# Linear attention, second pass: softmax work of a tile moved into the output products of the tile in front, and loads and sums at the pass boundary spread

## The chip, the cores and the metric

The kernel runs on one core of a Trainium2 chip. The metric is the device time of one execution in microseconds (us), the median of several runs. The core has a matrix engine (TensorE, PE in the profile; PEld is its weight loading), a vector engine (VectorE, DVE), a scalar engine (ScalarE, ACT), a general engine (GpSimd, POOL), and SyncE (SP), which here issues DMA transfers. Each engine works through its own queue in order and waits at an instruction until what it needs has been signalled.

## The reference

Four layers are applied to x (2048 rows of 512), each as a residual: A, B, A, B. Both layers A use one set of weights, both layers B another. The change lies in layer A:

```python
qkv = (x @ wqkv) ...                       # 32 heads of 16
pq = einsum(q, w_phi); pk = einsum(k, w_phi)
phi_q = concat([softmax(pq), softmax(-pq)])  # over the 16 features of a head
phi_k = concat([softmax(pk), softmax(-pk)])
kv = einsum(phi_k, v); z = sum(phi_k)        # over all 2048 rows
o = (phi_q @ kv) / (phi_q @ z + 1e-6)
x = x + o @ wo                               # x normalized (layernorm) before qkv
```

Layer B is a causal attention in four segments of 512 rows with a running memory; it follows each layer A.

## The kernel before, in words

Rows are worked in 16 tiles of 128. Products with full precision are made of three products of split operands (a high part and a low part), so a 128x512 projection is twelve matmuls over four blocks of the inner dimension.

Layer A has two passes. `pass1` (L746) goes through four segments of four tiles. It makes keys, values and query projections, the features of the keys, and adds up the key-value sums `kva` (`kv`, L825: 64 small matmuls for two tiles, then one addition on DVE). For most tiles the query projection is written to DRAM and comes back in the second pass (`load_q`, L956); for the last segment the queries stay on chip. The end of pass 1 is written out by hand (L893 to L954): two query and four key projections, two value tiles (the generator `rest`, steps 6 and 7), query projections of tiles 2 and 3, the two halves of the sums `kv(0)` and `kv(1)`, and the load of the output weights `awo` (eight DMAs of 256 KB; `pace()` at L458 makes SyncE wait for the last matmul issued so far). The output weights go into two of the four buffers `w8`, which also hold value weights and, for some segments, normalized rows.

The features of a tile are made in steps, each with a function of its own. `differences` (L638) subtracts the extremes of every head, two operations on POOL, into a tile of tag `P4`. `exp` (L648) is one operation on ACT. `scale_q` (L661) sums on DVE (`es`), makes a factor on DVE (`rr`) and multiplies half of the tile by it on POOL. After that PE can transpose the tile (`transposed`, L962, into `lg`, copied by ACT), and `products` (L976) multiplies it with the key-value sums and divides by the denominators on DVE (`r`, then `U`).

`pass2` (L992) goes through the 16 tiles. In step i of the loop, for a tile in the middle, the order of issue is: turn the output of tile i-1 (transposes on PE, casts on ACT, low parts on DVE), the exponential of tile i+2, the transposes of tile i+1, the products of tile i, the differences of tile i+3, sums and factor of tile i+2, the load of tile i+4, the load of the residual rows, and the twelve output products of tile i-1 with their addition on DVE and the store. Towards the end some steps handle two tiles at once (`NT - 5` and the like: step 10 makes the differences of tiles 13 and 14, step 11 those of tile 15).

Order is kept by hand: wrappers named `Ordered` chain all operations of DVE, ACT, POOL and SyncE in the order in which the program issues them, and `held` does so for PE. Generators yield between pieces, and the first 104 pieces of pass 2 are interleaved with the opening of the following layer B (`STEPS`, L47): its weight loads, the normalization of its first segment, in which POOL refines the root (`refine`, L380) and PE transposes the rows (`columns`, L393). The rest of pass 2 runs in early slots of layer B.

All operations on DVE, ACT, POOL and SyncE pass through one helper, so that the profile puts them at L155; matmuls stand at L177, transposes at L181 and L187.

Of the kernel before, what the change touches and what calls it, by code (L numbers as in the profile page):

```python
# [101 lines left out]
def interleave_kernel(ctx, tc, x_in, a_wqkv, a_wphi, a_wo, b_wq, b_wk, b_wv, b_wo, b_beta,  # L102
# [572 lines left out]
    class LayerA:  # L675
# [70 lines left out]
        def pass1(self, first):  # L746
# [44 lines left out]
            for n, s in enumerate(SEGS):  # L791
# [30 lines left out]
                    self.pqs[i] = dtile((P, D), nm("pq"))  # L822
                    sync.dma_start(out=self.pqs[i], in_=pq)

                def kv(t2, n=n, v=v, es=es):  # L825


                    pk = PS(("mx", "my")[t2], 1)[:, 0 : 8 * VW].rearrange("p (g e) -> p g e", e=VW)
                    for g in range(8):
                        for t in range(2 * t2, 2 * t2 + 2):  # L830
                            for j in range(4):
                                h = 4 * g + j
                                mm(pk[32 * j : 32 * j + 32, g, :], lhsT=es[t][:, 32 * h : 32 * h + 32],
                                   rhs=v[:, t, VW * h : VW * h + VW], start=(t == 2 * t2), stop=(t == 2 * t2 + 1),
                                   tile_position=(0, 32 * j))
                    yield
                    if n == 0 and t2 == 0:
                        dve.tensor_copy(kva, pk)
                    else:
                        dve.tensor_tensor(out=kva, in0=pk, in1=kva, op=ADD)  # L840
                    yield
# [65 lines left out]
                for i, (at, t) in enumerate(tiles):  # L907
                    for j, _ in enumerate(qproj(t, e, later) if at else kproj(t, e)):
                        if j == 2 and i > 1:
                            scaled(i - 2)  # L910
                        yield
                    if at:
                        begun(t)
                    if i > 0:
                        exp(e[sum(tiles[i - 1])])
                    if i == 2:
                        yield from late
                for i in (6, 7):
                    for j in range(4):
                        next(rest)  # L920
                        if j == 2:
                            scaled(i - 2)
                        yield
                    if i == 6:
                        exp(e[sum(tiles[i - 1])])
                        yield from kv(0)
                for _ in qproj(2, e, later):
                    yield
                begun(2)
                add = kv(1)  # L930
                next(add)
                pace()
                self.wo = load_w("awo")
                yield from add
                KN = self.KN = sp.tile([P, 8, 4, VW], F32, tag="KN", bufs=1, name=nm("KN"))
                den = kva[:, :, DH]
                dve.tensor_scalar(den, den, 0.5e-6, None, op0=ADD)
# [54 lines left out]
        def pass2(self):  # L992
# [2 lines left out]

            transposed = self.transposed
            self.rest = []
            for i in range(NT):
                soon = [i + 2] if i < NT - 5 else [i + 2, i + 3] if i == NT - 5 else [i + 3]
                soon = [n for n in soon if 2 < n < NT]  # L1000
                if i > 0:
                    if i <= NT - 4:
                        if i < NT - 4:
                            oT = turn_halves(self.o)
                        else:
                            oT = turn([self.o[:, c * P : (c + 1) * P] for c in range(NC)])
                        yield
                    for n in soon if i != 1 else ():
                        exp(self.e[n])
                    self.o = T2("ot", OT) if NT - 4 <= i else T2("U", UU)  # L1010
                    if i > 2:
                        yield from transposed(i + 1)
                    yield from self.products(i)
                for n in [i + 3] if i < NT - 6 else [i + 3, i + 4] if i == NT - 6 else [i + 4]:
                    if 3 < n < NT:
                        self.e[n] = differences(*self.raw.pop(n))
                for n in soon if i != 1 else ():
                    scale_q(self.e[n])
                for n in [i + 4] if i < NT - 7 else [i + 4, i + 5] if i == NT - 7 else [i + 5]:
                    self.load_q(n)  # L1020
                if i < NT - 4:
                    ahead = residual(self.xsrc, i, ("ot", OT))
                else:
                    self.rest.append(self.o)
                if 0 < i <= NT - 4:
                    steps = out_proj(x, self.xdst, i - 1, oT, self.wo, i < 3)
                    if i < 3:
                        for _ in range(2):
                            next(steps)
                            yield  # L1030
                        yield from transposed(i + 1)
                    if i == 1:
                        for n in soon:
                            exp(self.e[n])
                    yield from steps
                if i == 1:
                    scale_q(self.e[i + 2])
                x = ahead
# [622 lines left out]
```

## Time and profile before

| | us |
|---|---|
| median of three runs | 1315.0 (1313.81 to 1315.15) |
| the profiled execution: its own time | 1319.74 |
| its span | 1318.0 |
| PE busy | 1265.2 (96%) |
| PE weight load busy | 978.4 (74%) |
| DVE busy | 1078.5 (82%) |
| ACT busy | 836.6 (63%) |
| POOL busy | 753.7 (57%) |
| mean granted clock of PE | 0.995 |

The page of the profile counts busy time by engine and follows back the chain of work that ended last. In rows of the timeline, the columns are start, duration, engine, line, operation, output and inputs with their sizes, and a count where rows are merged; in brackets stands how long the engine was idle before it and what ended that. Rows of the chain have start, duration and what ran. In rows of the view by windows, each engine's busy time has its instruction count in brackets, and granted PE clock, share of the DMA engines and GB/s follow. Matmuls overlap, and their ends are modelled, so that a busy PE is not PE at its peak.

Names: `es` and `rr` are the sums and the factor of a query tile, `P` its features, `tb` and `mmq` a loaded query tile and its extremes, `lg` the transposed tile in PSUM, `KN` the key-value sums, `U` and `ot` the output of a tile, `oh` and `ol` its turned halves, `w` and `oh` in `g<-w,oh` the output products.

### The profile page before, as it was taken

The numbers are of one execution on the slowest core, as the hardware profiler recorded it, in microseconds if no ns is written. First come the engines' busy times: TensorE is split into PE (matmuls) and PEld (weight loads), VectorE is DVE, ScalarE is ACT, GpSimd is POOL, SyncE is SP. The second block draws the span as 40 slices with busy tenths as digits, with TensorE's granted clock in tenths as the row PEclk, the third lists the DMA queues.
The fourth block names the chain that finished last, engine by engine and source line by source line (L and its number), as shares of the span: only waits on it lengthen the run. The fifth ranks groups of instructions, "written<-read, shape, count | busy, mean of one in ns | idle before, by whom it ended". The sixth has DMA issues, their size and how long they took to land.

```text
span 1318.0 us, 42698 instructions
## 1 busy us (share of the span) xinstructions
PE 1265.2 (96%) x16832; PEld 978.4 (74%) x16832; DVE 1078.5 (82%) x3523; ACT 836.6 (63%) x1232; POOL 753.7 (57%) x1122
## 2 busy tenths in 40 slices
PE   8999989999999999999999999899999999999987
PEld 7887767777777777777668887677777777777765
DVE  5766858788998998998857768687899899898995
ACT  6546434547778788776644434464678868877754
POOL 0668845425657667666324447562356766766653
PEclk9999989999999999999999999899999999999999
DMA  6398167545555545545451101855546545544432
GB/s 211 110 354 268 62 203 232 169 120 145 182 172 140 160 120 145 159 134 156 130 168 57 65 34 53 266 181 158 143 129 209 174 127 152 144 131 119 122 83 81
DMA packets 134423, 196.64 MB, mean 149 GB/s; under 512 B 15440, under 2 KB 61648, under 8 KB 133456
## 3 DMA queue, kind: packets, MB, share of 16 engines
q1 hardware_dynamic: 133408, 193.80, 48.7%
q8 instruction: 134, 2.20, 0.7%
q14 instruction: 65, 0.53, 0.1%
q10 hardware_dynamic: 816, 0.11, 0.1%
HBM read 101.05 MB, written 39.85 MB: 107 GB/s over the span
## 4 chain that ended last, share of the span: by engine, by line
PE 69%; DVE 17%; DMA 4%; POOL 3%; SPq 2%; issue 2%; ACT 2%; DVEq 0%; POOLq 0%; ACTq 0%
PE g L177 54%; PE lg L177 6%; PE g L181 3%; PE mx L177 3%; DVE es L155 3%; DVE U L155 2%; POOL P L155 2%; SPq L155 2%; DVE g L155 2%; DVE mx L155 2%; PE my L177 1%; DVE my L155 1%; DMA w<-awo 1%; DMA wqk<-wqk 1%; DMA e<-ta 1%
## 5 line engine op out<-in xcount | busy, mean ns | idle before, releaser
L155 ACT ACTIVATE P<-lg 128x1024 f32<-128x1024 f32 x316 | 324.3, 1026 | 98.0 <-PE lg L177 77.1
L155 POOL TENSOR_SCALAR_AFFINE_SELECT P<-P 128x256 f32<-128x256 f32 (+1 forms) x448 | 189.9, 442 | 234.7 <-ACT P L155 207.8
L155 DVE CUSTOM_DVE_ANT_0 g<-g,mask 128x128 f32<-128x128 f32 (+3 forms) x392 | 189.5, 539 | 10.1 <-PE g L177 9.7
L155 DVE CUSTOM_DVE_ANT_0 mx<-mx,mask 128x512 f32<-128x512 f32 (+2 forms) x316 | 159.2, 504 | 42.1 <-PE my L177 33.8
L177 PE MATMUL g<-hh,wqk 64*128 64x512 f32 (+1 forms) x960 | 183.9, 393 | 4.2 <-SPq L155 2.5
L177 PE MATMUL g<-w,oh 64*128 64x512 f32 (+2 forms) x848 | 164.8, 384 | 8.2 <-DMA w<-awo 5.1
L155 DVE CUSTOM_DVE_ANT_0 my<-my,mask 128x512 f32<-128x512 f32 (+2 forms) x316 | 164.2, 520 | 0.0
L177 PE MATMUL lg<-e,e 64*128 64x512 f32 (+1 forms) x1010 | 146.2, 343 | 7.8 <-ACT P L155 7.8
L177 PE MATMUL g<-P,v 128*32 128x128 f32 (+3 forms) x2064 | 151.6, 433 | 0.1
L155 DVE DVE_READ_ACCUMULATOR2_ANT mxs<- 128x1 f32 x1024 | 145.1, 142 | 0.0
L177 PE MATMUL g<-w,hh 64*128 64x512 f32 (+1 forms) x672 | 142.1, 394 | 2.8 <-SPq L155 1.3
L177 PEld LDWEIGHTS lg<-e,e 64*128 64x128 f32 x1010 | 92.8, 184 | 52.6 <-ACT P L155 20.2
L177 PEld LDWEIGHTS g<-hh,wqk 64*128 64x128 f32 (+1 forms) x960 | 100.6, 185 | 23.6 <-SPq L155 4.8
L177 PEld LDWEIGHTS g<-w,oh 64*128 64x128 f32 (+1 forms) x848 | 95.3, 188 | 27.7 <-DMA w<-awo 6.6
L177 PEld LDWEIGHTS g<-P,v 128*32 128x32 f32 x2064 | 64.8, 109 | 61.3 <-issue 53.8
L155 ACT COPY tb<-g 128x512 f32<-128x512 f32 (+1 forms) x132 | 71.2, 576 | 53.9 <-PE g L177 53.6
L177 PE MATMUL g<-hl,wqk 64*128 64x512 f32 (+1 forms) x480 | 102.7, 390 | 0.0
L177 PE MATMUL g<-w,ol 64*128 64x512 f32 (+2 forms) x424 | 101.2, 381 | 0.0
L177 PEld LDWEIGHTS g<-w,hh 64*128 64x128 f32 (+1 forms) x672 | 83.5, 186 | 18.0 <-SPq L155 2.2
L177 PE MATMUL g<-w,hl 64*128 64x512 f32 (+1 forms) x336 | 88.8, 391 | 0.0
L155 POOL TENSOR_TENSOR ta<-tb,ta 128x512 fp32r<-128x512 f32 x60 | 76.2, 1290 | 16.3 <-ACT ta L155 13.3
L177 PE MATMUL mx<-e,e 63*128 63x256 f32 (+3 forms) x323 | 82.2, 318 | 2.4 <-DVE r L155 1.5
(170 smaller groups left out, 2937.7 us busy)
## 6 DMA issues: line engine op xcount, KB each, us to landing
e<-ta SPq DMA_DIRECT2D x384, 128.0 KB
wqk<-wqk SPq DMA_DIRECT2D x128, 256.0 KB
x<-x SPq DMA_DIRECT2D x48, 256.0 KB
pq<-tb SPq DMA_DIRECT2D x24, 256.0 KB
tb<-pq SPq DMA_DIRECT2D x24, 256.0 KB
x<-xr SPq DMA_DIRECT2D x22, 256.0 KB
xr<-x SPq DMA_DIRECT2D x20, 256.0 KB
x<-in SPq DMA_DIRECT2D x16, 256.0 KB
```

What stands on the lines that cost most here:

```text
L155: i = f(*a, **k)
L177: return held(nc.tensor.matmul(*a, **k))
L181: return held(nc.tensor.transpose(*a))
```

## The change

Three edits in layer A. Both layers A run them.

In `kv`, a new argument lets the sums of two tiles be made in two halves.

At the end of pass 1, each of the two value tiles starts with a `pace()` and the issue of half of the loads of the output weights. The sums of tiles 0 and 1 are made in two halves inside the second value tile, after its first and its third block; those of tiles 2 and 3 in two halves, one inside the query projection of tile 2 and one after it. Before, all sums of a pair were made in one piece, and all loads were issued behind the second pair.

In pass 2, from step 2 on, the exponential, the sums and the factor that step i+1 would have issued are issued in step i, ahead of the last block of its output products: in a step in the middle those of tile i+3 behind the differences of tile i+3 in that step. Step 2 still issues those of tile 4 at the old places as well. The differences, the transposes, the products and the loads of query tiles stay where they were.

```diff
-                def kv(t2, n=n, v=v, es=es):
+                def kv(t2, n=n, v=v, es=es, split=False):
...
+                        if split and g == 3:
+                            yield
...
+                self.wo = []
+                wsteps = bring(self.wo, "awo")
+                sums = [kv(t2, split=True) for t2 in range(2)]
                 for i in (6, 7):
+                    pace()
+                    for _ in range(2):
+                        next(wsteps)
                     for j in range(4):
                         next(rest)
                         if j == 2:
                             scaled(i - 2)
                         yield
+                        if i == 7 and j in (0, 2):
+                            next(sums[0])
+                            yield
                     if i == 6:
                         exp(e[sum(tiles[i - 1])])
-                        yield from kv(0)
-                for _ in qproj(2, e, later):
+                    else:
+                        yield from sums[0]
+                for j, _ in enumerate(qproj(2, e, later)):
+                    if j == 1:
+                        next(sums[1])
                     yield
                 begun(2)
-                add = kv(1)
-                next(add)
-                pace()
-                self.wo = load_w("awo")
-                yield from add
+                yield from sums[1]
+                for _ in wsteps:
+                    pass
...
+            def due(i):
+                soon = [i + 2] if i < NT - 5 else [i + 2, i + 3] if i == NT - 5 else [i + 3]
+                return [n for n in soon if 2 < n < NT]
+
             for i in range(NT):
-                soon = [i + 2] if i < NT - 5 else [i + 2, i + 3] if i == NT - 5 else [i + 3]
-                soon = [n for n in soon if 2 < n < NT]
+                soon = due(i) if i < 3 else ()
...
                     if i == 1:
                         for n in soon:
                             exp(self.e[n])
-                    yield from steps
+                        yield from steps
+                    else:
+                        for _ in range(1 if i == 2 else 3):
+                            next(steps)
+                            yield
+                        for n in due(i + 1):
+                            exp(self.e[n])
+                        for n in due(i + 1):
+                            scale_q(self.e[n])
+                        yield from steps
```

## The prediction

> **What bounds the kernel now.** I read the page first, then the chain of waits around the two places that the change touches, then the timelines of single engines there.
>
> ```profile
> span 1318.0 us, 42698 instructions
> PE 69%; DVE 17%; DMA 4%; POOL 3%; SPq 2%; issue 2%; ACT 2%; DVEq 0%; POOLq 0%; ACTq 0%
> ```
>
> Most of the chain is TensorE (PE), so an edit off PE counts only where PE waits. In the second pass it does. One tile there, in the chain of waits of the first layer A:
>
> ```profile
> 197.32 1.14 DVE es L155
> ...
> 199.21 1.07 POOL P L155
> 200.32 0.71 PE lg L187 x16
> ...
> 203.04 1.14 DVE es L155
> ```
>
> From `es` to the next `es` is 5.72 us, a closed loop: sums of tile i+2 (DVE), factor (POOL), transposes of that tile (PE), products of the tile before it behind them in PE's queue, division by the denominators (DVE), next sums. PE's own work in that tile is shorter:
>
> ```profile
> 200.32 0.71 PE L187 MATMUL lg<-ident,P 64*128 64x64 f32 x16 [0.53 <-POOL P L155]
> 202.05 0.73 PE L177 MATMUL g<-w,oh 128*128 128x512 f32 x2
> 205.06 0.27 PE L187 MATMUL mx<-ident,U 64*128 64x64 f32 x1
> 206.03 0.71 PE L187 MATMUL lg<-ident,P 64*128 64x64 f32 x16 [0.51 <-POOL P L155]
> ```
>
> The twelve output products take 202.05 to 205.06, 3.0 us. The wait ahead of the transposes is 0.51, so PE is busy 5.2 of 5.72 us. No way of moving the sums can win more than 0.5 us a tile.
>
> The other place is the start of the second pass, where PE waits for the output weights:
>
> ```profile
> 170.74 4.51 SPq L155 DMA_DIRECT2D w<-awo  x8
> 177.57 1.38 PE L177 MATMUL g<-w,oh 128*128 128x512 f32 x3
> 181.66 1.65 PE L177 MATMUL g<-w,oh 128*128 128x512 f32 x3 [2.71 <-DMA w<-awo]
> 187.14 0.36 PE L187 MATMUL mx<-ident,U 64*128 64x64 f32 x1
> 815.46 4.41 SPq L155 DMA_DIRECT2D w<-awo  x8
> 822.29 0.74 PE L177 MATMUL g<-w,oh 128*128 128x512 f32 x2
> 825.92 1.65 PE L177 MATMUL g<-w,oh 128*128 128x512 f32 x3 [1.62 <-DMA w<-awo]
> 831.40 0.36 PE L187 MATMUL mx<-ident,U 64*128 64x64 f32 x1
> ```
>
> The first four rows are the first layer A, the others the second. The clock fell with the wait; in the view by windows the third number from the end is the granted PE clock, 0.66:
>
> ```profile
> 180.00:190.00 10.00, 8.34 (x70) 6.09 (x71) 2.99 (x7) 3.58 (x5) 2.70 (x4) 0.66 0.68 242
> ```
>
> **Part 1: output weights earlier.** Between the first output product of tile 0 and the next tile's turn (177.57 to 187.14) stand twelve products and one tile's transposes: 3.0 + 0.65 = 3.65 us of work took 9.57. The excess is 5.9 us, 2.7 of it waiting and 3.2 mostly the low clock. In the second layer A: 831.40 - 822.29 - 3.65 = 5.5 us.
>
> In the first layer the eight loads now go out in two lots from the last key projection on, two value tiles and a query projection (twelve products, 3.0 us each) ahead of the old place: 9 us earlier, longer than PE waits, so all 5.9 us come back. In the second, the four `w8` buffers hold the value weights and the normalized rows until the last value product (both operands are `w` in the row below), so SyncE's loads stand waiting for it, and so would anything behind them on that queue; nothing is, until pass 2's first load of query rows.
>
> ```profile
> 808.27 3.04 PE L177 MATMUL g<-w,w 128*128 128x512 f32 x12
> 812.20 1.52 POOL L155 TENSOR_TENSOR P<-P,es 128x512 f32<-128x512 f32 x1 [1.48 <-DVE es L155]
> 814.03 1.27 PE L177 MATMUL my<-v,P 128*32 128x17 f32 x128
> ```
>
> The last value product ends near 811.3 in either order, 4 us ahead of the old first issue. Old, the last weight landed 10.5 us after the first issue (815.46 to 825.92); new, that gives 821.8, ahead of PE's need at 822.3 (823.5 with part 2). So that wait goes too; if the loads took 2 us longer, half of it would stay.
>
> **Part 2: key-value sums spread.** They are the same products. The first half of tiles 2 and 3's sums now stands after six of the twelve products of the next query projection and needs the scaled tile that POOL finishes at 812.20 + 1.52 = 813.72. PE gets there near 812.6, waits 1.1, and still has both halves of the sums (0.6 each) and six products (1.5) to do: it ends near 816.4 where the old sums ended at 815.3. So +1.2 in the second layer (0 if POOL is earlier, +2 if the query projection's later steps slip as well); in the first PE is idle around these sums already, and I take nothing. Part 1 and 2 together: -5.9 - 5.5 + 1.2 = -10.2 us.
>
> **Part 3: exponential, sums and factor one tile ahead.** The old loop is cut: the factor is ready a tile before the transposes ask. But look at POOL's queue. It runs in order. In tile i it subtracts the extremes of tile i+3 (two operations), and, old, then multiplied by the factor of tile i+2. Now the exponential of tile i+3 (ScalarE), its sums (DVE) and its factor (POOL) all follow the subtraction of the same tile in the same step, and the subtraction of tile i+4 is queued behind that factor. That is a new closed loop. The trace has all its links in one run, in the first pass:
>
> ```profile
> 144.18 2.09 POOL P L155 x2
> 146.30 1.07 ACT P L155
> 147.39 1.23 DVE es L155
> ```
> ```profile
> 149.37 1.06 POOL L155 TENSOR_TENSOR P<-P,rr 128x512 f32<-128x512 f32 x1 [0.95 <-DVE rr L155]
> 150.40 1.06 POOL L155 TENSOR_TENSOR P<-U,mm 128x512 f32<-128x512 f32 x1
> ```
>
> Subtraction to next subtraction: 150.40 - 144.18 = 6.22 us, against 5.72 old. DVE passes the delay on: the addition that ends each tile's output rows, and the low halves of the next, are queued behind the sums that wait for the exponential; PE then waits before the output products, about 1 us a tile (6.22 less its 5.2). On ScalarE the exponential now stands ahead of the next turn's two casts, which need PE's turn behind the output products and so come no earlier; that adds nothing.
>
> Length of the stage, from the turn of tile 1 to the transposes of tile 13. Old:
>
> ```profile
> 191.74 1.02 ACT L155 COPY P<-lg 128x1024 f32<-128x1024 f32 x1 [2.39 <-PE lg L187]
> 223.86 0.49 POOL L155 TENSOR_TENSOR st<-st 128x4 f32<-128x4 f32 x2 [0.59 <-ACT st L155]
> 225.49 1.06 POOL L155 TENSOR_TENSOR P<-tb,mmq 128x512 f32<-128x512 f32 x1
> 246.73 0.71 PE L187 MATMUL lg<-ident,P 64*128 64x64 f32 x16 [0.41 <-POOL P L155]
> 891.26 0.71 PE L187 MATMUL lg<-ident,P 64*128 64x64 f32 x16 [0.40 <-POOL P L155]
> ```
>
> 246.73 - 187.14 = 59.6 us, and 891.26 - 831.40 = 59.9 in the second layer. New: tile 5's exponential follows the copy at 191.74, so 1.02 + 1.09 (146.30 to 147.39) + 1.98 (147.39 to 149.37) + 1.03 later POOL starts the subtraction of tile 6 at 196.86, 9.7 after the turn. From there seven rounds of 6.22 bring it to tile 13: 43.5. The refinement of layer B's norm, six small operations, stands once in POOL's queue: 225.49 - 223.86 = 1.6. After that comes the double step of tiles 13 and 14, where the chain runs on through DVE and PE:
>
> ```profile
> 247.21 0.69 DVE L155 TENSOR_TENSOR hl<-g,hh 128x512 fp32r<-128x512 f32 x1
> 247.81 0.68 DVE L155 TENSOR_TENSOR ot<-g,ot 128x512 f32<-128x512 f32 x1
> 270.54 1.22 DVE L155 TENSOR_REDUCE es<-P 128x64 f32<-128x1024 f32 x1
> 272.35 0.69 DVE L155 CUSTOM_DVE_ANT_0 g<-g,mask 128x512 f32<-128x512 f32 x1
> ```
>
> Both subtractions take 4.2 (twice 2.09), the second exponential 1.1, the sums of tile 14 1.8 (270.54 to 272.35, sums and factor), three more 128x512 operations on DVE at 0.6 from start to start 1.8, then on PE twelve products 3.0 and the turn 0.5 (5.2 less 3.0 less the 1.7 from 200.32 to 202.05): 12.4. New stage 9.7 + 43.5 + 1.6 + 12.4 = 67.2: +7.6 and +7.3, +15 in both layers. In return the sums of tile 15, the row at 270.54, leave the opening of layer B, where DVE has no pause:
>
> ```profile
> 270.00:280.00 10.00, 9.95 (x88) 7.01 (x90) 9.72 (x38) 3.26 (x5) 3.52 (x3) 1.00 0.21 65
> ```
>
> At most 1.8 us a layer (DVE is busy 9.72 of 10), nothing if PE (9.95) is the limit; I take -1, -2 in both.
>
> **The clock.** The low clock of the 0.66 row came with a wait of 2.7 us and cost up to 3.2 beyond it. The new stage makes two such holes a layer: behind the refinement, 1.0 + 1.6 = 2.6 us, and behind the double step, about 3. Part of PE's slowness there goes into its 1 us of slack. I take one fall a layer at 1.5: +3 (ends 0 and +12.8, four falls at full price). [...]
>
> **Sum.** -10.2 + 15 - 2 + 3 = +5.8 us. Against the profiled execution's own 1319.74 (span 1318.0) that is 1325.5; the median of the three runs, 1315.0, lies 4.7 lower, and I carry the difference over: 1320.8, or 1321.
>
> **Rivals.** *A, POOL does not hold the loop* (the subtraction runs ahead of the factor, or the exponential is issued late enough that neither loop closes). Then PE's 5.2 us decide: nine tiles at -0.5 in two layers, -9, with -10.2 and -2: 1294, about 1296 with some loss at the close. For it: the edit does cut the old loop. Against: all POOL operations are chained in the order of the program. It decides from a POOL round under 5.7 us. This is the case on the other side, faster. 0.17.
> *B, the loop binds but the close is cheap*: if tiles 10 to 12 hide the double step, a layer loses seven times 0.5 and little more, 4 us: -10.2 + 8 - 2 = -4, 1311. 0.13.
> *C, the clock falls twice a layer* at nearly full price: +10 in place of +3, about 1328. For it: the one wait of this size that is quoted brought a fall. 0.20.
> *E, the clock stays whole*: PE's holes are cut short by the work that fills them (transposes, turn), and the term of 3 is nothing: -10.2 + 15 - 2 = +2.8, 1318. For it: the holes are an estimate from sums of links, each of which may overlap a little more. 0.15. [...]
> *D, the change does not do what it says* in the second layer, the loads finding no buffer before the sums: then its 5.5 stay lost, 1326.5; I put it inside C's range. Late loads of the query rows, which POOL already waits for in places, would lengthen some rounds by up to a microsecond; also inside.
> Forecast itself (the loop binds, one fall a layer): 0.35, with its own range of 1314 to 1326.
>
> **Numbers.** Range 1309 to 1331: it takes in B, E, the forecast and C, and leaves out A and little else. A measurement of this kernel can tell about 0.2%, 2.6 us, from no change. Faster by more (under 1312.4): A and part of B, 0.22. Within it: part of E, the lower end of the forecast and the rest of B, 0.14. Slower: 0.64.
>
> **What would show it.** The waits for `w<-awo` gone at both places and the clock whole there. In the second pass, POOL's subtractions 6.2 us apart, with an idle stretch ahead of each factor, and PE's wait moved from the transposes (for POOL) to the output products (for DVE). The stage from turn 1 to transposes 13 near 67 us; sums of tile 15 before layer B opens; a clock under 1 in the last tiles. I am wrong if tiles are 5.2 to 5.7 us apart, or if PE's waits are not on that path.

## The result and the profile after

| | before | after |
|---|---|---|
| median, us | 1315.1 (1313.81 to 1316.16, 4 runs) | 1325.5 (1322.36 to 1327.33, 4 runs) |
| ratio, 95% interval | | 1.0077 [1.0055, 1.0099] |
| profiled execution, own time | 1319.74 | 1325.99 |
| span | 1318.0 | 1324.1 |
| mean granted clock of PE | 0.995 | 0.995 |

The change makes the kernel 10.4 us slower. Its page gives the span and the shares of the chain:

```profile
span 1324.1 us, 42698 instructions
PE 73%; DVE 13%; POOL 5%; ACT 3%; DMA 2%; issue 2%; SPq 1%; DVEq 0%; POOLq 0%; ACTq 0%
```

DMA fell from 4% to 2% of the chain, and about half of that is the row of the output weights (`w<-awo`), which had 1.1% of the span before and is gone. POOL rose from 3% to 5%.

**The pass boundary.** From the timelines of SyncE and PE, first layer A, then the second:

```profile
157.50 4.66 SPq L155 DMA_DIRECT2D w<-awo  x8
167.43 0.67 PE L177 MATMUL my<-v,P 128*32 128x17 f32 x56 [1.07 <-POOL P L155]
177.72 1.67 PE L177 MATMUL g<-w,oh 128*128 128x512 f32 x6
181.54 0.27 PE L187 MATMUL mx<-ident,U 64*128 64x64 f32 x1
812.42 4.39 SPq L155 DMA_DIRECT2D w<-awo  x8
815.44 0.67 PE L177 MATMUL my<-v,P 128*32 128x17 f32 x56 [1.23 <-POOL P L155]
825.72 1.67 PE L177 MATMUL g<-w,oh 128*128 128x512 f32 x6
829.56 0.27 PE L187 MATMUL mx<-ident,U 64*128 64x64 f32 x1
```

The six first output products now run in one piece. The turn of tile 1 starts at 181.54, where it started at 187.14: 5.6 us won. In the second layer it is 829.56 against 831.40; this layer's start came 1.7 us late, so 3.5 are won there. PE's new wait of about a microsecond for the scaled key tile stands in both layers.

**The second pass.** POOL's timeline in the first layer A (`P<-P,rr` is the factor, `P<-tb,mmq` the first subtraction of the next tile):

```profile
190.43 1.06 POOL L155 TENSOR_TENSOR P<-P,rr 128x512 f32<-128x512 f32 x1 [1.48 <-DVE rr L155]
191.44 1.06 POOL L155 TENSOR_TENSOR P<-tb,mmq 128x512 f32<-128x512 f32 x1
...
196.62 1.06 POOL L155 TENSOR_TENSOR P<-P,rr 128x512 f32<-128x512 f32 x1 [3.10 <-DVE rr L155]
...
211.32 1.06 POOL L155 TENSOR_TENSOR P<-tb,mmq 128x512 f32<-128x512 f32 x1 [1.25 <-DMA tb<-pq]
```

In a plain round the factors follow each other at 6.19 us, with POOL idle about 3 us (2.99 to 3.10) ahead of each: it has subtracted tile i+3, and waits for ScalarE and DVE to bring the same tile's factor, while the next subtraction is queued behind that. Once in the first layer and twice in the second (0.41 and 1.17 us) the subtraction also waits for its query tile. The chain shows why that one is late:

```profile
202.58 0.69 DVE xr L155
...
203.29 2.39 DMA x<-xr
...
206.12 5.06 DMA tb<-pq
...
211.32 1.06 POOL P L155
```

The load of the next query tile stands on SyncE's queue behind the store of a finished row tile, and that store waits for the addition (`xr`) that now stands behind a newer tile's sums on DVE.

From tile 5 on PE no longer waits for POOL at the transposes. It waits in the output products (PE's timeline, holes in brackets), 0.94 us in a plain round and about 2 us where a load was late or two tiles are made at once:

```profile
203.98 0.51 PE L177 MATMUL g<-w,ol 128*128 128x512 f32 x1 [0.94 <-DVE ol L155]
...
217.67 0.50 PE L177 MATMUL g<-w,ol 128*128 128x512 f32 x1 [1.86 <-DVE ol L155]
...
246.26 1.03 PE L177 MATMUL g<-w,oh 128*128 128x512 f32 x2 [2.12 <-DVE ot L155]
...
251.94 0.71 PE L187 MATMUL lg<-ident,P 64*128 64x64 f32 x16
```
```profile
900.31 0.71 PE L187 MATMUL lg<-ident,P 64*128 64x64 f32 x16
```

The last two rows are the transposes of tile 13 in either layer. From the turn of tile 1 to them it is now 251.94 - 181.54 = 70.4 us and 900.31 - 829.56 = 70.75, where it was 59.6 and 59.9.

**The clock.** The view by windows, PE alone; the number right behind the count in brackets is the granted clock:

```profile
216.00:218.00 2.00, 0.33 (x1) 1.00 0.25 83
218.00:220.00 2.00, 2.00 (x8) 0.78 0.76 152
220.00:222.00 2.00, 2.00 (x21) 0.50 0.82 229
```

PE stood still for most of 216 to 218 (the hole of 1.86), and from about 219.1 the clock was halved for 3.4 us. In the profiled execution this happened three times in the first layer A (near 219, 233 and 246) and once in the second (895), and no longer at the output weights, where before it had happened twice, for 6.8 us each.

### The profile page after: what moved, and what is told of

Its sections match the earlier page's. It is cut to its first block, busy times and chain, and to the rows that moved or that the text cites. A ratio compares the mean times of both kernels' runs of the same rounds, so it can differ in the third digit from the quotient of the medians.

```text
span 1324.1 us, 42698 instructions
## 1 busy us (share of the span) xinstructions
PE 1265.9 (96%) x16832; PEld 977.8 (74%) x16832; DVE 1076.3 (81%) x3523; ACT 837.9 (63%) x1232; POOL 753.9 (57%) x1122
## 4 chain that ended last, share of the span: by engine, by line
PE 73%; DVE 13%; POOL 5%; ACT 3%; DMA 2%; issue 2%; SPq 1%; DVEq 0%; POOLq 0%; ACTq 0%
PE g L177 58%; PE lg L177 6%; POOL P L155 4%; PE g L181 3%; PE mx L177 3%; DVE es L155 2%; ACT P L155 2%; DVE g L155 2%; DVE U L155 1%; PE my L177 1%; DMA tb<-pq 1%; DVE mx L155 1%; DVE my L155 1%; SPq L155 1%; DVE rr L155 1%
## 5 line engine op out<-in xcount | busy, mean ns | idle before, releaser
L155 ACT ACTIVATE P<-P 128x1024 f32<-128x1024 f32 x64 | 68.0, 1062 | 58.4 <-POOL P L155 58.2
L155 DVE TENSOR_REDUCE es<-P 128x64 f32<-128x1024 f32 x64 | 77.6, 1213 | 28.8 <-ACT P L155 28.7
```

The lines of the kernel that those rows point to most:

```text
L155: i = f(*a, **k)
```

## The experiments

The theory after the result: the boundary wins what was forecast, and the second pass loses more than that, because POOL stands in a closed loop of 6.19 us. Rivals for the second pass: the late query loads are the real bound; DVE's order, with sums ahead of the addition and of the low parts, is; the holes only cost because the clock falls behind them; the last tiles, where two sums stand together, cost as much as the loop. All ratios are to the kernel before, with 95% intervals; 0.001 is 1.3 us.

**1. The pass boundary alone** (`pass2` as before the change):

```diff
-                soon = due(i) if i < 3 else ()
+                soon = [i + 2] if i < NT - 5 else [i + 2, i + 3] if i == NT - 5 else [i + 3]
+                soon = [n for n in soon if 2 < n < NT]
...
-                        for _ in range(1 if i == 2 else 3):
-                            next(steps)
-                            yield
-                        for n in due(i + 1):
-                            exp(self.e[n])
-                        for n in due(i + 1):
-                            scale_q(self.e[n])
-                        yield from steps
+                    yield from steps
```

> The end of pass 1 as changed (early output weights, spread key-value sums), the second pass as before. Theory 1 (the prediction's sum: this half gains about 10 us, the second pass loses more than that through POOL's queue): 1305, 10 us under the kernel before, no wait for the output weights, clock whole there, tiles of the second pass 5.72 us. Theory 2 (the loads were hidden in unprofiled executions, so this half gains little, and the second pass loses only about 10): 1313 to 1316.

Measured: 1304.3 us, ratio 0.9933 [0.9918, 0.9949]: 8.8 us faster. Its tiles run as they did before, 5.72 us apart with PE waiting for POOL at the transposes:

```profile
200.97 0.71 PE L187 MATMUL lg<-ident,P 64*128 64x64 f32 x16 [0.51 <-POOL P L155]
206.69 0.71 PE L187 MATMUL lg<-ident,P 64*128 64x64 f32 x16 [0.51 <-POOL P L155]
```

**2. The second pass alone** (loads and sums as before the change):

```diff
-                wsteps = bring(self.wo, "awo")
-                sums = [kv(t2, split=True) for t2 in range(2)]
...
+                add = kv(1)
+                next(add)
+                pace()
+                self.wo = load_w("awo")
+                yield from add
```

> The second pass as changed, the end of pass 1 as before. Theory 1: 1315 + 15 to 20 = 1330 to 1335, with POOL's subtractions 6.2 us apart. Theory 2: 1325, the same as with both halves.

Measured: 1332.7 us, ratio 1.0147 [1.0126, 1.0169]: 19.3 us slower. The two parts are additive: 0.9933 times 1.0147 is 1.0079, the whole change 1.0077. So the first theory has the sign right: the second pass loses about twice what the boundary wins.

**3. The factor behind the next differences.** Only POOL's order is turned: `factor_q` issues a tile's sums and factor on DVE as before and returns POOL's multiplication, which is issued in the next step, after the subtraction of the next tile.

```diff
                         self.e[n] = differences(*self.raw.pop(n))
+                for f in todo:
+                    f()
+                todo = []
...
                         for n in due(i + 1):
-                            scale_q(self.e[n])
+                            todo.append(factor_q(self.e[n]))
```

> Both halves as changed, but the factor's multiplication on POOL is issued one step later, behind the next subtraction; sums and exponential stay where the change put them. Theory 1 (POOL's queue order closes the loop): the loop opens, tiles go to PE's 5.2 to 5.4 us, and with the gain at the end of pass 1 the time is 1296 to 1302. Theory 3 (the loss comes from the sums on DVE standing ahead of the addition and low halves, not from POOL): tiles stay near 6.2 us and the time at 1323 to 1328.

Measured: 1320.3 us, ratio 1.0058 [1.0041, 1.0075], 2.5 us under the change's 1.0077, with intervals that overlap, and between both expectations. POOL's timeline shows that its loop is open and another one has closed:

```profile
197.18 1.06 POOL L155 TENSOR_TENSOR P<-tb,mmq 128x512 f32<-128x512 f32 x1 [4.76 <-DMA tb<-pq]
...
202.08 1.06 POOL L155 TENSOR_TENSOR P<-tb,mmq 128x512 f32<-128x512 f32 x1 [1.81 <-DMA tb<-pq]
...
210.03 1.06 POOL L155 TENSOR_TENSOR P<-tb,mmq 128x512 f32<-128x512 f32 x1 [4.73 <-DMA tb<-pq]
```

The factors hardly wait any more (0.19 us at most in these rounds); the subtractions wait for their query tiles. The timelines of DVE and SyncE have the reason:

```profile
200.38 1.22 DVE L155 TENSOR_REDUCE es<-P 128x64 f32<-128x1024 f32 x1 [3.13 <-ACT P L155]
...
202.13 0.69 DVE L155 TENSOR_TENSOR xr<-g,xr 128x512 f32<-128x512 f32 x1
```
```profile
202.85 0.32 SPq L155 DMA_DIRECT2D x<-xr  x1
203.22 1.94 SPq L155 DMA_DIRECT2D x<-x  x4
205.25 0.38 SPq L155 DMA_DIRECT2D tb<-pq  x1
```

The query load at 205.25 stands behind the store at 202.85. The store waits for the addition (`xr`, 202.13), which stands behind sums (`es`, 200.38) that wait, through the exponential, for the subtraction of the tile two before it: from 197.18 to 210.03, 12.85 us for two tiles.

**4. The factor's multiplication on DVE, from step 2 on:**

```diff
-    def scale_q(e):
+    def scale_q(e, eng=pool):
...
-        pool.tensor_tensor(out=e[:, :, 1, :], in0=e[:, :, 1, :],
+        eng.tensor_tensor(out=e[:, :, 1, :], in0=e[:, :, 1, :],
...
-                            scale_q(self.e[n])
+                            scale_q(self.e[n], dve)
```

> Both halves as changed, but from step 2 on the factor is multiplied in on DVE instead of POOL (0.7 us more on DVE, 1.0 less on POOL in each tile). Theory 1: POOL's loop is open; DVE is at some 5.0 us a tile, so tiles of 5.2 to 5.7 us and 1298 to 1308. Theory 3: DVE's order holds the tile, which gets longer by the 0.7: about 6.9 us and 1335.

Measured: 1336.5 us, ratio 1.0178 [1.0159, 1.0197], the slowest of all. The time is the one expected by the theory of DVE's order, about 1335, but its rounds of 6.9 us are not there: in the first layer the rounds from tile 4 to tile 9 take between 4.98 and 11.68 us. POOL, now free of factors, again waits for loads, longer than in experiment 3:

```profile
199.84 1.06 POOL L155 TENSOR_TENSOR P<-tb,mmq 128x512 f32<-128x512 f32 x1 [7.46 <-DMA tb<-pq]
...
205.18 1.34 POOL L155 TENSOR_TENSOR P<-tb,mmq 128x512 f32<-128x512 f32 x1 [3.26 <-DMA tb<-pq]
...
214.29 1.06 POOL L155 TENSOR_TENSOR P<-tb,mmq 128x512 f32<-128x512 f32 x1 [6.63 <-DMA tb<-pq]
```

From 199.84 to 214.29 two tiles take 14.45 us. The multiplication (0.69 us and more) now stands ahead of the addition too, inside the same loop through the loads.

**5. Factor late, and each query load one step earlier:**

```diff
-                for n in [i + 4] if i < NT - 7 else [i + 4, i + 5] if i == NT - 7 else [i + 5]:
+                for n in [4, 5] if i == 0 else [i + 5] if i < NT - 8 else [i + 5, i + 6] if i == NT - 8 else [i + 6]:
                     self.load_q(n)
```

> As the run with the factor multiplication behind the next differences (ratio to the kernel before 1.0058), with each load of query features issued one step earlier in the second pass. Theory 1 (two loops, one behind the other: first GpSimd's own loop of 6.19 us a tile, and once that is opened the loop over two tiles that runs query load, differences, exponential, sums, addition, store on SyncE's queue, next query load): both are open now, the tiles fall to between PE's own 5.2 us and the 5.7 us of the kernel before, PE's waits on ol behind VectorE stay at or below 0.7 us, no row of GpSimd waits on tb<-pq for over 0.5 us, and the ratio is 0.988 to 0.994, which is that of the change without its second pass (0.9933) or below it. Rival (VectorE's order is the bound: the sums stand ahead of the addition and of the low parts whatever releases them): tiles stay at 5.9 to 6.2 us, ratio 1.002 to 1.008.

Measured: 1310.1 us, ratio 0.9974 [0.9958, 0.9991]: 11.0 us less than experiment 3 (1.0058 - 0.9974 = 0.0084) from one line. Both loops are open as far as PE can see, and it runs four tiles in a row without a wait. POOL still waits for some query tiles, up to 2.72 us, where not over 0.5 was expected, but PE does not feel it:

```profile
211.10 0.66 PE L187 MATMUL lg<-ident,P 64*128 64x64 f32 x16
...
216.19 0.66 PE L187 MATMUL lg<-ident,P 64*128 64x64 f32 x16
```

These two are 5.09 apart, the three rounds ahead of them 4.99 to 5.00. But the ratio expected was 0.988 to 0.994. PE's timeline has the rest at the close:

```profile
238.64 0.71 PE L177 MATMUL g<-w,oh 128*128 128x512 f32 x2 [2.19 <-DVE ot L155]
...
244.79 0.71 PE L187 MATMUL lg<-ident,P 64*128 64x64 f32 x16
```

and DVE's timeline the cause:

```profile
234.25 1.22 DVE L155 TENSOR_REDUCE es<-P 128x64 f32<-128x1024 f32 x1 [0.27 <-ACT P L155]
...
236.00 1.21 DVE L155 TENSOR_REDUCE es<-P 128x64 f32<-128x1024 f32 x1
...
237.81 0.68 DVE L155 TENSOR_TENSOR ot<-g,ot 128x512 f32<-128x512 f32 x1
```

The sums of tiles 13 and 14 stand together ahead of one addition, which frees the accumulator for the next products. The last round takes 10.09 us in the first layer (with a clock fall behind the hole) and 8.51 in the second (without one), against 6.02 in experiment 1.

**6. The loads one step earlier, nothing else** (the line of experiment 5 in the changed kernel).

> The changed kernel with each load of query features of the second pass issued one step earlier, nothing else. Theory 1 (GpSimd's loop of subtraction, exponential, sums, factor is the first bound): the factor rows stay 6.19 us apart, and only the waits of 1.25, 0.41 and 1.17 us on tb<-pq go, with perhaps one fall of the clock: 1 to 5 us less than the changed kernel, ratio to the kernel before 1.004 to 1.008. Rival (the late loads are the bound, and the loop on GpSimd only fills what they leave): tiles at 5.7 us or less, ratio 0.993 to 0.998.

Measured: 1325.4 us, ratio 1.0091 [1.0067, 1.0114], no gain over the change. The loads no longer wait, and POOL's loop stands as it was:

```profile
209.29 1.06 POOL L155 TENSOR_TENSOR P<-P,rr 128x512 f32<-128x512 f32 x1 [2.99 <-DVE rr L155]
215.50 1.06 POOL L155 TENSOR_TENSOR P<-P,rr 128x512 f32<-128x512 f32 x1 [3.10 <-DVE rr L155]
```

The transposes of tiles 5 to 10 are 6.19 to 6.22 us apart, every one, in both layers. That settles the order of the two bounds: POOL's loop first, the loads behind it. The 1 to 5 us that the theory expected did not show in the times: in the traces the stretch from tile 5 to tile 10 is 1.5 and 1.7 us shorter than in the changed kernel, but from tile 10 to tile 13 the transposes take 25.5 us in its first layer, and 25.0 in the changed kernel.

Experiments 5 and 6 differ in POOL's order alone. From the transposes of tile 4 to those of tile 13 it is 62.0 and 61.7 us in experiment 6, and 54.8 and 53.3 in experiment 5: 15.6 us for both layers in the traces, and 15.3 between the medians. That is what POOL's order costs once the loads are early; 1.6 us of it may be the fall of the clock that one of experiment 5's two closes was spared.

**7. The last tile's sums back at their old place:**

```diff
-                soon = due(i) if i < 3 else ()
+                soon = due(i) if i < 3 or i == NT - 4 else ()
...
-                        for n in due(i + 1):
+                        for n in due(i + 1) if i + 1 < NT - 4 else ():
                             exp(self.e[n])
-                        for n in due(i + 1):
+                        for n in due(i + 1) if i + 1 < NT - 4 else ():
                             scale_q(self.e[n])
```

> The changed kernel with exponential, sums and factor of the last tile at their old place, behind the transposes of tile 12, all other tiles as changed. Theory 1 (the change takes the sums and the exponential of tile 15 out of layer B's opening, where VectorE was what the chain ran through, and so regains 2 us a layer there by the forecast; the trace shows 3.5 to 4.0 regained along layer B): the last tile's transposes come 1 to 2 us earlier, and layer B's opening gives up 2 to 4 us: in all 0 to 4 us more than the changed kernel, ratio to the kernel before 1.008 to 1.011. Rival (what layer B regains is slack of another kind, a clock that holds or waits that were covered anyway): 2 to 4 us less than the changed kernel, ratio 1.005 to 1.006.

Measured: 1325.0 us, ratio 1.0091 [1.0067, 1.0115]: inside the range of the first theory (1.008 to 1.011), and the interval leaves out the rival's (1.005 to 1.006). But it is not to be told from the change either: the difference is 0.0014, and with both intervals about 0.0033 either way. So what tile 15's sums are worth at one place or the other is not shown.

**8. Factor on DVE, loads one step earlier** (the lines of experiments 4 and 5).

> As the run with the factor multiplication on VectorE (ratio 1.0178), with each load of query features issued one step earlier. Theory 1 (there the bound was the loop over two tiles through the query loads: GpSimd waited 7.46, 3.26, 6.63 and 1.91 us on tb<-pq, a pair of tiles took 14.5 us): the waits go, the tiles take 5.2 to 5.9 us, and the ratio falls to 0.992 to 1.000. Rival (VectorE's own order, with 0.69 us more of work ahead of the addition, sets 6.9 us a tile): the waits on tb<-pq go, but PE's waits on ol stay at 1.5 us or more, and the ratio stays at 1.012 or above.

Measured: 1324.0 us, ratio 1.0082 [1.0061, 1.0103], 12.6 us better than experiment 4. The ratio lies between the two expectations, and each theory holds half. Three rounds in a row take 4.99 us in the first layer, so late loads were a bound in experiment 4. But POOL still waits 6.05 and 3.15 us for two query tiles around the start of these rounds, and rounds with DVE's holes stand on either side (PE's timeline):

```profile
194.25 0.50 PE L177 MATMUL g<-w,ol 128*128 128x512 f32 x1 [2.41 <-DVE ol L155]
...
217.62 0.50 PE L177 MATMUL g<-w,ol 128*128 128x512 f32 x1 [1.60 <-DVE ol L155]
```

**9. The second of the two tiles at the close behind the addition:**

```diff
-                        for n in due(i + 1):
+                        for n in due(i + 1)[:1]:
                             exp(self.e[n])
-                        for n in due(i + 1):
                             scale_q(self.e[n])
                         yield from steps
+                        for n in due(i + 1)[1:]:
+                            exp(self.e[n])
+                            scale_q(self.e[n])
```

> The changed kernel with one thing else: in the step that takes two tiles (13 and 14), the second tile's exponential, sums and factor are issued behind that step's output products and their addition, no longer ahead of them. Theory 1 (at the close two reductions and their factors stand ahead of one addition on VectorE, PE finds the accumulator of the next output products not free and waits 2.12 us and then 0.40 us, and the clock falls behind this hole in both layers): the wait of 2.12 us on ot goes in both layers, the last tiles come 2 to 4 us earlier in each, and the ratio to the kernel before falls by 3 to 8 us' worth, to 1.002 to 1.006. Rival (tiles 13 to 15 are held by GpSimd's loop, and the hole only shows that loop's length at another place): the hole moves behind the transposes or the low parts, and the ratio stays at 1.007 to 1.010.

Measured: 1324.7 us, ratio 1.0077 [1.0063, 1.0090]: the rival. The wait of 2.12 us for `ot` fell to 0.38 in both layers, but a hole of 2.20 us ahead of the products with the low parts took its place. The last round takes 10.02 us in the first layer (9.56 in the changed kernel), with a fall of the clock behind that hole, and 8.45 in the second (9.73), where the same hole brought none.

**10. All three repairs** (experiments 3, 5 and 9 together).

> The three repairs in one kernel: factor multiplication behind the next differences, query loads one step earlier (these two together gave 0.9974, with tiles 4.99 us apart and without a wait of PE in four rounds, but the double step then held PE for 2.19 and 0.46 us in both layers), and the second tile of the double step behind that step's addition. Theory 1: the double step's hole goes, 3 to 4 us a layer with the clock's fall behind it, and the ratio is 0.990 to 0.9945, at or below that of the change without its second pass (0.9933). Rival (what the tiles gain is given back in the layer behind, whatever stands at the close): 0.996 to 0.999.

Measured: 1310.8 us, ratio 0.9964 [0.9952, 0.9975], against 0.9974 without the split of the close. That is in the rival's range, though what the tiles gain is given back at the close and not in the layer behind. Here the moved hole can be read, on PE and on DVE:

```profile
236.46 0.70 PE L177 MATMUL g<-w,oh 128*128 128x512 f32 x2 [0.38 <-DVE ot L155]
239.44 0.64 PE L177 MATMUL g<-w,ol 128*128 128x512 f32 x1 [2.27 <-DVE ol L155]
...
244.42 0.71 PE L187 MATMUL lg<-ident,P 64*128 64x64 f32 x16
```
```profile
235.63 0.68 DVE L155 TENSOR_TENSOR ot<-g,ot 128x512 f32<-128x512 f32 x1
...
236.83 1.21 DVE L155 TENSOR_REDUCE es<-P 128x64 f32<-128x1024 f32 x1
...
238.64 0.42 DVE L155 TENSOR_TENSOR ol<-mx,oh 128x256 fp32r<-128x256 f32 x1
```

The addition is early now, the second sums stand behind it, and the low parts of the next turned tile behind the sums: the hole of 2.19 us went from one operand of PE to the next. The last round of the first layer is 10.09 us as before, that of the second 11.33, with a fall of 6.8 us. In the first layer, four rounds take 5.0 to 5.1 instead of 5.7 to 5.85, but the one ahead of them 6.18, the three behind them 6.1 to 6.4, and the last 10.09 instead of 6.02: the nine rounds from tile 4 to tile 13 take 54.9 us, against 52.1 in experiment 1. So the second pass with both loops opened is still no better than the old one.

**11. The loads moved, the sums not spread** (on experiment 1):

```diff
-                sums = [kv(t2, split=True) for t2 in range(2)]
...
+                        yield from kv(0)
...
+                add = kv(1)
+                next(add)
                 for _ in wsteps:
                     pass
+                yield from add
```

> The change without its second pass (0.9933), and with the key-value sums at their old place in one piece each, so that only the output weights' loads are moved. Theory 1 (the loads alone take away the two waits on w<-awo; spreading the sums gives nothing that the path sees, and in layer 2 the loads stand behind a value product, so that the forecast charged 1.2 us there to the whole of it): 0 to 2 us from the run with spread sums, ratio 0.991 to 0.996. Rival (the spreading covers the exponential and factor of the key tiles, PE would wait for POOL P there without it): PE waits of over 0.5 us for POOL P or ACT P ahead of the sums, 2 to 5 us more, ratio 0.995 to 0.998.

Measured: 1310.9 us, ratio 0.9965 [0.9952, 0.9978], 4.2 us behind experiment 1 (0.0032, and with both intervals about 0.0020 either way). So spreading the sums is worth something, against the theory, though not for the reason that the rival gave. PE's timeline and the windows of the first layer:

```profile
172.56 0.19 PE L177 MATMUL my<-v,P 128*32 128x17 f32 x1 [2.75 <-issue]
```
```profile
174.00:176.00 2.00, 2.00 (x5) 0.50 0.00 0
```

The last product of the second pair of sums starts 2.75 us after the one in front of it, with no wait that the profile shows, and the clock is halved for 6.8 us from 172.1 on, still inside that hole. At this boundary experiment 11 falls 3.8 us behind experiment 1 in its trace; in the second layer it gains 0.5. In the kernel before the same place shows 1.37 us. The trace has one clue: in both runs a packet of 16 KB on the queue that the view of the DMA lists as `instruction` lands 1.3 us before the hole ends (at 171.28 and 169.12). The trace does not say what the packet is for, so that what PE waited for there is not shown.

**12. The refinement of layer B's first norm on DVE:**

```diff
-            return norm_T(self.xsrc, s, self.hT[s], slow=True, off=True)
+            return norm_T(self.xsrc, s, self.hT[s], slow=True, off=s > 0)
```

> The changed kernel with the refinement of layer B's first norm on VectorE, no longer on GpSimd between two factors. Theory 1 (the refinement's 1.63 us stand inside GpSimd's loop once in each layer: the factor rows are 7.84 us apart there, 222.69 to 230.53): that distance falls to 6.2 us, with PE's waits of 1.14 and 1.16 us behind it: 1.5 us a layer, 3 us in all, ratio to the kernel before 1.004 to 1.008. Rival (the loop has slack there because VectorE holds PE at the close anyway, and what comes earlier waits at the double step): 0 to 1 us, ratio 1.007 to 1.010; the same if the refinement on VectorE pushes sums and additions back by what GpSimd gains.

Measured: 1324.7 us, ratio 1.0066 [1.0052, 1.0081], not to be told from the change (1.0077). The time lies in the first theory's range, but the distance that it is about does not: the factors around the refinement came to 7.05 us apart, from 7.84, where 6.2 was expected. The refinement's first pair of operations alone took 2.08 us on DVE,

```profile
224.01 2.08 DVE L155 TENSOR_TENSOR st<-st 128x4 f32<-128x4 f32 x2
```

ahead of the division by the denominators and the next sums. Each of the two lasts until a subtraction on POOL ends (225.07 and 226.09, POOL's 225.05 and 226.07, and the same in the second layer); the next pair of the same size, with POOL idle, takes 0.17 us each. What POOL gained, DVE's order gave back in part.

## Why the prediction was right, and where its sizes were off

The forecast was 1321.0 in a range of 1309 to 1331, slower with 0.64; the time is 1325.5.

**The loop.** Forecast 6.22 us from subtraction to subtraction, measured 6.19, and 6.20 to 6.21 in experiment 6, except for the round with the refinement, 7.83. The signs named for it are there: POOL idle ahead of each factor, and PE's wait moved from the transposes to the output products. That wait is 0.94 us in a plain round, where the prediction had about 1. Experiments 5 and 6 together show the loop as the cause: they differ in POOL's order alone, and the rounds from tile 5 to tile 9 are 4.98 to 5.11 us in one and 6.19 to 6.22 in the other. Rival A (POOL does not hold the loop) is excluded by the trace, and experiment 5 shows that its 5.2 us a tile were to be had, with two more edits. That the loop through the loads stood right behind POOL's, so that opening POOL's alone wins little (experiment 3), the prediction did not see.

**The pass boundary.** Forecast -10.2; the trace gives -5.6 and -3.5, the times of experiment 1 -8.8 [-10.8, -6.7]. In the second layer PE was to wait 1.1 us for POOL's scaled tile: 1.23. In the first, where the prediction took nothing, the same wait is 1.07. The price of the spread sums has the right sign in the second layer, where the first output product comes 1.8 us later against the start of the layer (forecast 1.2, with 2 as its upper end). In the first layer, where the prediction took nothing, they are a gain: without them experiment 11 is 3.8 us slower there.

**The second pass.** This is the term that was too small. Forecast for the stage 9.7 + 43.5 + 1.6 + 12.4 = 67.2 us; measured in the first layer 9.9 (turn at 181.54 to the subtraction at 191.44), 46.3 (to the first subtraction of tile 13 at 237.75) and 14.2 (to 251.94). The middle is 43.5 + 1.6 and the load wait of 1.25; in the second layer 46.7, with load waits of 0.41 and 1.17. The prediction named late loads of query rows and left them out of the sum. The close, 12.4, measured 14.2 in both layers. Of the excess a clock fall explains 1.6: that is what the last rounds of the two layers differ by in experiment 5, 10.09 with a fall and 8.51 without, and in experiment 9, 10.02 and 8.45. So the stage costs 10.8 and 10.85 us a layer, 21.7, where the prediction had 15 and 3 for the clock. Of the 3.7 between them 2.8 are the three load waits; the first step (9.9 for 9.7) and the close without its fall (12.6 for 12.4) are 0.4 each over both layers.

**The clock.** Forecast one fall a layer that counts, behind holes of 2.6 us at the refinement and about 3 at the double step. The holes are 1.14 and 1.16 at the refinement (1.32 and 1.16 in the second layer) and 2.12 at the double step. There were three falls and one; two of the first layer's lie in rounds that POOL's loop sets, where PE has slack, and cost nothing there: the factors stay 6.19 and 6.20 us apart through both. One fall a layer at the close is what the sum should hold, and did, at 1.5 us for a measured 1.6.

**The opening of layer B.** Forecast -1 a layer. Comparing the start of the same instructions in the changed kernel and in experiment 1, whose second pass is the old one: the lag falls from 10.8 to 9.5 us over the first layer's opening, and from 21.8 to 21.4 in the second. By the end of the two layers B 0.7 and 0.3 of it are left. Experiment 7 could not see it in the times.

**The carry-over from the profiled execution.** The sum was made against 1319.74 and gave 1325.5; the changed kernel's profiled execution took 1325.99. That these two meet is luck: two errors cancel in it. The working is too small: with what was measured for each term it is -9.1 + 21.7 - 1.7 = +10.9, or +11.6 with what is left at the ends of the layers B, near the 10.4 between the medians and not the 5.8 of the sum. And the profiled execution of before had lost time that has nothing to do with the change: compared with it instruction by instruction, the change, experiment 1 and experiment 2 all gain 3.4 to 4.0 us along the first layer B and 3.2 to 4.1 along the second, although experiment 1 changes nothing there. About 1 us of the first is one place, where PE waited 0.81 us for a load (`e<-ta`, at 381.52) that came in time in the others; the rest lies at many places, and its cause is open. So taking off 4.7 us to come to the median fits, and what was off in size is the second pass, 21.7 us for 15 + 3, mostly by load waits that the prediction had seen in the trace and left out of its sum.

**The rivals.** B, a cheap close, is excluded by its 14.2 us, and E, a whole clock, by the falls at it (though five holes of 2.0 to 2.5 us in the experiments brought none). C, two falls a layer, gave 1328: there were four in all, but two of them cost nothing. D, loads that find no buffer in the second layer, is excluded by the six first output products there, which run without a wait. Of the rivals named after the result, late loads and DVE's order are real bounds, but behind POOL's: the loads show once that loop is open (experiment 3), and DVE's order at the close (experiments 5, 9 and 10).

## What to carry to other kernels

Where an operation is moved ahead on one engine, follow every queue that its new place stands in, and draw the loops through several of them: here the first was POOL's own (6.19 us), the second ran through DVE's addition, the store on SyncE and the next load (6.4 us a tile), the third was DVE's sums ahead of PE's operands at the close. Opening either of the first two alone gave 2.5 us or nothing (experiments 3 and 6), both together 13.5 (1.0077 to 0.9974); the third was moved, not opened. Look at what stands behind a wait: here POOL stood idle for 2.99 to 3.10 us ahead of each factor, with the subtraction that feeds the next one queued behind. Cut a change that mixes two ideas in two and time both: here the half that nobody doubted, loads and sums (0.9933), is the best version found, ahead of the kernel before and of all repairs of the other half (0.9964).

## What the runs showed of the hardware

In the fourteen profiled executions the clock fell 36 times ahead of PE's last product, to half (0.50 in the windows) and for 3.4 or 6.8 us, and not behind every hole. Each fall began within or up to 3.0 us behind a hole of PE; the table sorts all holes of PE behind the first 20 us by length and counts those with a fall.

| hole of PE, us | holes | with a fall |
|---|---|---|
| 2.5 and more (longest 3.58) | 9 | 9 |
| 2.0 to 2.5 | 22 | 17 |
| 1.5 to 2.0 | 21 | 6 |
| 1.0 to 1.5 | 130 | 4 |
| 0.85 to 1.0 | 105 | 0 |

Of the four between 1.0 and 1.5, three had a second hole close by. The same hole went either way: 1.86 us brought a fall in the first layer of the changed kernel and none in the second, and 2.2 us did so in the first layers of experiments 5 and 9 and not in their second layers. A fall of 3.4 us at the close, a place without slack, cost 1.6 us (the last rounds of experiment 5, 10.09 and 8.51); in rounds that POOL's loop sets it cost nothing (the factors of the changed kernel stayed 6.19 and 6.20 us apart). Of the 36 falls 32 came with holes of 1.5 us and more, and no hole between 0.85 and 1.0 us brought one.

In these runs the same kernel's time went with its clock. Over all 40 runs of the kernel before that were made beside the experiments, the run with a mean clock of 1.000 took 1307.6 us and those at 0.994 took 1314.0 to 1318.3; a line through all gives 1.2 us for each 0.001 (0.5 to 1.3 in the three groups of runs that they come from). Experiment 1 had 0.998 to 1.000 in all six runs, and a narrow spread (1303.7 to 1305.8). Its trace has no fall, and no hole of PE over 1.44 us.

In experiment 12 two operations of 128x4 elements on DVE took 1.06 and 0.99 us, each up to the end of a subtraction on POOL, and the next pair of this size took 0.17 us each with POOL idle.
